# Layer A's third and fourth values unit as seven Strassen products, with sums made ahead

## The chip, the cores and the metric

One Trainium2 chip, one of its cores. The metric is the device time of one execution in microseconds; the median of three runs is given, and one further execution was taken with the hardware profiler. All matrix work runs on TensorE (PE), which keeps its order of instructions as the program wrote it; VectorE (DVE), ScalarE (ACT), GpSimd (POOL) and the queue of SyncE (SP) do the same with theirs.

## The reference

Two attention layers on 2048 rows of 1024 channels, 32 heads of 32, in float32; the outputs stand side by side.

```python
# layer A: a dilated window of 8 keys, step 2
qkv = (x @ wqkv).reshape(B, S, 3, H, Dh)
idx = pos[:, None] - off[None, :]            # off = 0, 2, ..., 14
logits = einsum("bhsd,bhswd->bhsw", q, kg) * Dh ** -0.5
o = einsum("bhsw,bhswd->bhsd", softmax(logits), vg)
a = o.reshape(B, S, D) @ wo
# layer B: causal, the last 256 keys
scores = einsum("bhqd,bhkd->bhqk", q, k) * Dh ** -0.5
b = einsum("bhqk,bhkd->bhqd", softmax(masked scores), v).reshape(B, S, D) @ wo
out = concatenate([a, b], -1)
```

## The kernel before

**Units.** The 2 x 2048 rows are cut into eight units of 512: units 0 to 3 are layer B (dense attention), units 4 to 7 layer A (windows). Each unit needs queries and keys (`qk_items`: eight slots s = 0..7 of four heads, two products each of 24 matmuls), values (`v_items`), attention (`attention`, `window`) and the output projection. Every float32 operand is split into a high and a low float32r part (`Stream.parts`: a cast on ACT or DVE, then one subtraction on DVE for each 512 columns), and a product is three matmuls: high x high, high x low, low x high.

**Who sets the order.** The Python code holds a planner: a clock with costs of its own (`Clock`), one list of matrix work `gemm` in the order of `plan`, and lists of attention work. Its loop takes from these whatever the clock says is ready first, and what it takes goes into the program in that order. Work for other engines is put into their queues when the clock passes a due time (`ck.defer`). Whatever a constant moves there, it moves the order of instructions of every engine after it. The chip doesn't know the clock: there each engine waits at the head of its queue.

**Weights and other operands.** `items` is the one sequence of 512 KB loads, issued on POOL's queue (L176) into three `raw` tiles; a tile is loaded again when its split is done. Some items have a gate: they are loaded only when the planner believes that their data stand in DRAM.

**Values before (L556 to 634).** Each unit makes its values as 512 x 1024 by 1024 x 1024, in three parts: part 0 (slots 0 to 3 of the attention) by 96 matmuls of 512 columns, parts 1 and 2 (slots 4, 5 and 6, 7) by 96 matmuls of 256 columns each; nine items of weights. A window unit has part 0 in slot 0, part 1 in slot 5 and part 2 in slot 7 (`V_SLOTS`). A finished bank is copied to `vbuf` by ACT or DVE (L621, L624).

**Strassen products before.** The output projection of layer A is made at the end, two units together, as seven products of half size in place of eight (`PRODUCTS`, `product`), 48 matmuls each: first units 4 and 5, then 6 and 7. Their sums of attention outputs (`sd`) and of weights (`td`) are made in the background: `background` (L845) reads two tiles of 512 KB on SP, runs four additions of 128 x 512 on DVE (L860), writes 2 x 512 KB back (L866). Two such tasks may run at once, in slots 4 to 7 of a pool of ten tiles `r`. The additions are put into DVE's queue 1.5 us (`BG_SLACK`) after the planner's landing time of the loads. Eight of these tasks concern outputs and four the weights `wo` (`weight_sums`).

**Windows.** For each slot of a layer A unit: scores (128 small matmul records into `s`), mask, maximum, exponent, sum and transpose (L946 to L976 on DVE), spreading on ACT (L985, L988), the product with the values into `o`, and a copy to `r` (L1047) that is written to DRAM as `od`. Queries and keys reach their seats `pbuf` by DMAs on SP's queue.

**Dense rows.** In units 0 to 3, `log_sum` (L1123) makes a small tile `hl` on DVE, and one matmul `s<-ident,hl` turns it.

Of the kernel before, what the change touches and what calls it, by code (L numbers as in the profile page):

```python
# [7 lines left out]
F32 = mybir.dt.float32  # L8
# [22 lines left out]
EXTRA, EACH = 246, 5.2  # L31
P_LATE = 1.5
VPARTS = ((0,4),(4,2),(6,2))
V_SLOTS = {0:0,5:1,7:2}
# [4 lines left out]
PRODUCTS = (("11", "11"), ("12", "21"), (0, 3), (2, 2), ("22", 1), (3, 0), (1, "22"))  # L39
PAIRS = (6,)  # L40
O_LATE = {4: {2: (0, 1), 3: (2, 3)}, 5: {2: (4, 5), 3: (6, 7)}}
O_AT = {}
BG_REST, BG_SLACK = 2.0, 1.5
C1, C3, CG, CV = 0.108, 0.2, 0.231, 0.242
# [192 lines left out]
def kernel(ctx, tc, xs, wqk, wv, wo, outs, units):  # L237
# [38 lines left out]
    for u in range(U):  # L276
        for s in range(NG):
            if 0 < u <= DU:
                plan += [("o", u - 1, n) for n in (O_SLOTS if u < DU else O_LATE[u]).get(s, ())]
            elif u in O_LATE:  # L280
                plan += [("o", DU - 1, n) for n in O_LATE[u].get(s, ())]
            if (u, s) in O_AT:
                plan.append(("p", DU, O_AT[u, s]))
            plan.append(("qk", u, s))
            vs = V_SLOTS if u else V0_SLOTS
            if s in vs:
                plan.append(("v", u, vs[s]))
        if u + 1 < U:
            plan.append(("x", u + 1))
# [3 lines left out]
    sd = {u: dram.tile([P, 4, 4, S], F32, name=f"sd{u}") for u in range(DU, U, 2)}  # L293
    td = dram.tile([P, 4, 4, S], F32, name="td")
    done = {}
    for k in ("stack", "v", "o", "ot", "out", "nat", "second", "clear", "scores", "s", "t"):
        done[k] = {}
# [5 lines left out]
    def product_items(u, i):  # L303
# [12 lines left out]
        for j in range(2):  # L316
            key = ("p", u, i, "t", j)
            if isinstance(b, str):
                n, c = 4 * (int(b[1]) - 1) + 2 * j, S * (int(b[0]) - 1)
                item(key, "w", wo[units[u][0], n:n + 2, :, c:c + S].rearrange("n p c -> p n c"))  # L320
            else:
                item(key, "w", td[:, b, 2 * j:2 * j + 2, :])
                gates[where[key]] = landed("t", 2 * j, 2 * j + 1)

# [13 lines left out]
    for p in plan:  # L338
# [3 lines left out]
        elif p[0] == "p":  # L342
            product_items(p[1], p[2])
        elif p[0] == "v":
            s0, n = VPARTS[p[2]]
# [23 lines left out]

    st.gates = gates  # L370
    where_o = {"ot": 0, "s": 0, "bg": 0}

# [105 lines left out]
    def qk_items(u, s):  # L478
# [100 lines left out]
        for t in range(2):  # L579
# [15 lines left out]
            def run(k, t=t, h=h):  # L595
# [6 lines left out]
                then = where["qk", u, s, t] + 1  # L602
                if k == ASK and then < len(st.items) and st.items[then][0] != "x":
                    st.split_to(then + 1)
                if k in (4, 6) and then < len(st.items) and st.items[then][0] in ("xw", "xt"):
                    st.split_to(then + k // 2)
# [100 lines left out]
    def o_items(u, n):  # L707
# [27 lines left out]
        def after(k):  # L735
            if k == NK - 1:
                done["out"][u, n] = True
                for f in list(stores.values()):
                    f()
                if u == DU - 1 and n == NG - 1:  # L740
                    ck.defer(ck.now + 3.0, weight_sums)
                o = stp.tile([P, S], F32, tag="ost", name="ost")
# [11 lines left out]

    held, totals = {}, {}

    def product(u, i):
# [38 lines left out]
        def after(n, k):  # L796
# [11 lines left out]
            def store(r, col, tile, e):  # L808
                def go():
                    nc.scalar.dma_start(outs[ORDER[u + r], 4 * col + n], tile)  # L810
                    ck.load("store", e)
                ck.defer(e, go)

            if i in (1, 4):
                where_o["ot"] += 1
                o = band[where_o["ot"] % 2][:, 1024:1536] if where_o["ot"] % 3 else stp.tile([P, S], F32, tag="ost", name="ost")
            if i == 0:
# [26 lines left out]

    bg = {"tasks": [], "idle": [0, 1]}  # L845

    def background():
# [28 lines left out]

        ck.defer(e + BG_SLACK, add)
        background()
# [4 lines left out]

    def weight_sums():
        w = wo[units[DU][0]]
        for n in range(4):
            task([(2 * i, w[n + 4 * i].rearrange("p (a b) -> p a b", a=2)) for i in range(2)],
                 ((0, 2, 0, ALU.subtract), (2, 3, 2, ALU.subtract), (3, 3, 0, ALU.subtract), (1, 1, 3, ALU.subtract)),
                 td[:, :, n, :], "t", n)

    def output_sums(u, k):
        task([(2 * r, od[u + r][:, k::4, :]) for r in range(2)],
             ((3, 2, 3, ALU.add), (2, 0, 2, ALU.subtract), (0, 3, 0, ALU.subtract), (1, 1, 0, ALU.subtract)),
             sd[u][:, :, k, :], "s", (u, k))
# [137 lines left out]
    def clear(buf):  # L1032
# [7 lines left out]
        done["clear"][buf] = ck.use("pool", 2.5, ck.now)  # L1040

    def finish(u, s, h):
        hg = u * NG + s
        done["o"][hg] = ck.now
        if u >= DU:
            o = slot(2 + hg % 2)[:, :S]
            nc.scalar.copy(o, h["o"])  # L1047
# [33 lines left out]
    def attention(u, s):  # L1081
# [43 lines left out]
        def log_sum():  # L1125
# [4 lines left out]
            def parts():  # L1130
# [135 lines left out]
    for p in plan:  # L1266
# [18 lines left out]
        elif p[0] == "p":  # L1285
            gemm += product(p[1], p[2])
    gemm = [Item(r, lambda run=run, after=after: (run(), after)[1], c) for r, run, c, after in gemm]

# [86 lines left out]
```

## Time and profile before

| | us |
|---|---|
| median of three runs (lowest, highest) | 1815.52 (1812.15, 1817.01) |
| the profiled execution, own time | 1813.28 |
| span of its trace | 1811.5 |
| PE busy | 1788.4 |
| DVE busy | 1265.9 |
| ACT busy | 918.4 |
| POOL busy | 410.0 |

The span runs from the first instruction to the last; 1.8 us of the execution's own time lie around it. PE's busy time counts pipelined matmuls from their start to a modelled end, so what one matmul costs in a stream is read from the distance of starts. By the copies L1047, which end each window, unit 4 runs from about 1033 us, unit 5 from 1175, unit 6 from 1353, unit 7 from 1513, and from 1671 only Strassen products are left.

### The profile page before, as it was taken

The numbers are of one execution on the slowest core, as the hardware profiler recorded it, in microseconds if no ns is written. First come the engines' busy times: TensorE is split into PE (matmuls) and PEld (weight loads), VectorE is DVE, ScalarE is ACT, GpSimd is POOL, SyncE is SP. The second block draws the span as 40 slices with busy tenths as digits, with TensorE's granted clock in tenths as the row PEclk, the third lists the DMA queues.
The fourth block names the chain that finished last, engine by engine and source line by source line (L and its number), as shares of the span: only waits on it lengthen the run. The fifth ranks groups of instructions, "written<-read, shape, count | busy, mean of one in ns | idle before, by whom it ended". The sixth has DMA issues, their size and how long they took to land. (4 is left out here: it accounts for less than half of the span.)

```text
span 1811.5 us, 38626 instructions
## 1 busy us (share of the span) xinstructions
PE 1788.4 (99%) x14730; PEld 1461.1 (81%) x14730; DVE 1265.9 (70%) x2794; ACT 918.4 (51%) x2297; POOL 410.0 (23%) x950
## 2 busy tenths in 40 slices
PE   8999999999999999999999999999999999999999
PEld 6787777888777888778887788888888878888887
DVE  6677876768867769767678566646765767558866
ACT  5556466555656565656655344423542534345342
POOL 2313423222242223332224300101010011002220
PEclk9999999999999999999999999999999999999999
DMA  8455664645646556554636353546753675448884
GB/s 244 114 146 134 184 167 137 168 137 138 184 140 175 148 138 172 139 157 138 152 111 172 99 153 107 174 131 215 238 181 110 196 248 161 129 148 300 304 271 145
DMA packets 129240, 303.60 MB, mean 168 GB/s; under 512 B 16160, under 2 KB 31520, under 8 KB 129056
## 3 DMA queue, kind: packets, MB, share of 16 engines
q0 software_dynamic: 45216, 164.65, 30.4%
q1 hardware_dynamic: 73472, 116.56, 22.9%
q10 hardware_dynamic: 10368, 19.93, 3.0%
q8 instruction: 117, 1.92, 0.5%
q14 instruction: 67, 0.55, 0.1%
HBM read 189.79 MB, written 44.04 MB: 129 GB/s over the span
## 5 line engine op out<-in xcount | busy, mean ns | idle before, releaser
L269 PE MATMUL g<-x,w 128*128 128x512 f32 x3744 | 927.1, 394 | 7.5 <-DVE w L227 4.6
L269 PEld LDWEIGHTS g<-x,w 128*128 128x128 f32 x3744 | 692.8, 189 | 145.6 <-issue 6.6
L269 PE MATMUL g<-w,x 128*128 128x256 f32 (+1 forms) x2304 | 391.4, 320 | 0.4 <-DVE w L227 0.2
L227 DVE TENSOR_TENSOR w<-raw,w 128x512 fp32r<-128x512 f32 x518 | 339.6, 697 | 34.3 <-ACT w L221 27.5
L269 PEld LDWEIGHTS g<-w,x 128*128 128x128 f32 x2304 | 332.3, 190 | 28.5 <-issue 1.7
L1114 ACT ACTIVATE s<-s,nm 128x384 f32<-128x384 f32 (+2 forms) x512 | 274.6, 537 | 101.5 <-DVE nm L1109 101.3
L1109 DVE CUSTOM_DVE_ANT_0 s<-s,mask_d 128x384 f32<-128x384 f32 (+2 forms) x512 | 261.8, 555 | 88.0 <-PE s L269 87.4
L1173 POOL TENSOR_SCALAR_AFFINE_SELECT pbuf<-pbuf 128x128 f32<-128x128 f32 (+1 forms) x606 | 220.2, 391 | 325.9 <-ACT pbuf L1194 324.5
L1194 ACT ACTIVATE pbuf<-s 128x384 f32<-128x384 f32 (+2 forms) x480 | 202.9, 505 | 72.2 <-PE s L269 70.7
L269 PE MATMUL g<-r,w 128*128 128x512 f32 x768 | 191.5, 394 | 1.5 <-ACT r L1069 0.7
L269 PEld LDWEIGHTS g<-r,w 128*128 128x128 f32 x768 | 141.8, 188 | 31.3 <-DVE r L1073 1.6
L176 POOL DMA_DIRECT2D raw<-wqk x126 | 68.2, 541 | 434.4 <-DVE w L227 316.0
L224 DVE CAST w<-raw 128x1024 fp32r<-128x1024 f32 x196 | 135.6, 692 | 32.7 <-PE g L269 29.5
L269 PEld LDWEIGHTS s<-qst,kst 128*128 128x128 f32 x704 | 113.1, 188 | 40.8 <-ACT s L1114 16.3
L269 PE MATMUL s<-kst,qst 96*128 96x384 f32 (+2 forms) x512 | 142.6, 342 | 1.0 <-ACT s L1114 0.6
L269 PE MATMUL s<-qst,kst 128*128 128x256 f32 (+2 forms) x704 | 136.5, 302 | 3.5 <-ACT s L1114 3.0
L946 DVE TENSOR_TENSOR band<-s,near 128x160 f32<-128x160 f32 x128 | 32.5, 317 | 119.4 <-PE s L269 119.4
L269 PEld LDWEIGHTS s<-kst,qst 96*128 96x128 f32 x512 | 93.4, 189 | 26.1 <-issue 4.4
L1114 ACT ACTIVATION_READ_ACCUMULATOR s<-s,nm 128x1 f32 x512 | 105.4, 206 | 0.0
L176 POOL DMA_DIRECT2D raw<-wv x72 | 45.9, 638 | 237.5 <-DVE w L227 155.8
L985 ACT COPY wide<-band 32x512 f32<-32x512 f32 x128 | 79.0, 617 | 40.1 <-DVE band L976 37.9
L269 PE MATMUL o<-pbuf,vbuf 128*32 128x384 f32 (+2 forms) x1408 | 92.2, 391 | 0.0
(79 smaller groups left out, 1258.6 us busy)
## 6 DMA issues: line engine op xcount, KB each, us to landing
raw<-wqk POOLq DMA_DIRECT2D x126, 512.0 KB, 4.4
raw<-wv POOLq DMA_DIRECT2D x72, 512.0 KB, 5.1
qst<-nat SPq DMA_DIRECT2D x96, 256.0 KB, 4.7
kst<-nat SPq DMA_DIRECT2D x96, 256.0 KB, 5.8
raw<-wo POOLq DMA_DIRECT2D x44, 512.0 KB, 4.5
raw<-xs POOLq DMA_DIRECT2D x28, 512.0 KB, 4.7
outs<-ost ACTq DMA_DIRECT2D x37, 256.0 KB, 2.7
kst<-halo SPq DMA_DIRECT2D x72, 128.0 KB, 4.5
```

What stands on the lines that cost most here:

```text
L176: (self.nc.scalar if early else self.nc.gpsimd).dma_start(raw if len(ap.shape) == 2 else raw.rearrange("p (a b) -> p a b", a=2), ap)
L224: nc.vector.tensor_copy(t[:, 0, :], raw)
L227: nc.vector.tensor_tensor(t[:, 1, c:c + 512], raw[:, c:c + 512], t[:, 0, c:c + 512].bitcast(F32), op=ALU.subtract)
L269: nc.tensor.matmul(out, left, right, **k)
L946: nc.vector.tensor_tensor(p64()[:, j, :, 24:], banks[j][0][:, :160].rearrange("p (b c) -> p b c", b=4), m, op=ALU.add)
L985: nc.scalar.copy(diag[r:r + 32, :, :, c:c + 32], turned[r:r + 32, :, :, 1, :])
L1109: nc.vector.tensor_tensor_reduce(ps[:, :n], ps[:, :n], mask[:, cut:full], scale=-1.0, scalar=BIG, op0=ALU.add, op1=ALU.min, accum_out=nm)
L1114: nc.scalar.activation(ps[:, :n], ps[:, :n], AF.Exp, bias=nm, scale=-1.0, accum_out=sm)
L1173: nc.gpsimd.affine_select(w, w, pattern=[[0, m], [step, n]], compare_op=ALU.is_ge, fill=0.0, base=base, channel_multiplier=chan)
L1194: nc.scalar.activation(w, ps[:, :pack * n].rearrange("p (j n) -> p j n", j=pack), AF.Exp)
```

## The change

The values of units 6 and 7 are made together as seven Strassen products in place of `v_items`: left operands are quarters of the two units' `x` or sums of them, right operands quarters of `wv` or sums of them. Products 0 and 1 stand in slot 0 of unit 6, product 2 in slot 1, 5 in slot 2, 6 in slot 3, 3 in slot 7, and 4 in slot 0 of unit 7 (`VP_AT`). Results gather in four `r` tiles and go by DVE additions into `vbuf`; the right half of unit 7 goes through DRAM (`vd`) and is read back by SP (`value_load`).

The sums for it, and the weight sums `td` that the background made, are made by a chain of 24 steps (`half_sums`) that starts with the end of the dense layer: four loads of 128 KB on SP into one tile, `VSLACK` = 5 us after their planned landing four additions of 128 x 256 on DVE, one store of 512 KB on SP, then the next step. Eight steps make `tv` (sums of `wv`), eight `sx` (sums of `x`), eight `td`.

Three further edits: `HL_LATE` puts the turning matmul of `hl` 0.8 us later in the planner's time; the output sums of units 4 and 5 begin only when product 3 of the values is through, with 8 us (`BG_EARLY`) in place of 1.5 between planned landing and additions; the copies of finished windows use one `r` tile in two halves in place of two tiles.

```diff
+HL_LATE = 0.8
+VPAIR = 6
+VP_AT = {(6, 0): (0, 1), (6, 1): (2,), (6, 2): (5,), (6, 3): (6,), (6, 7): (3,), (7, 0): (4,)}
+SUMS_FROM = 31
+VREST, VLAST, VNEED, VSLACK = 0.5, 2.0, 3.0, 5.0
...
-BG_REST, BG_SLACK = 2.0, 1.5
+BG_REST, BG_SLACK, BG_EARLY = 2.0, 1.5, 8.0
...
-            if s in vs:
+            if s in vs and u < VPAIR:
                 plan.append(("v", u, vs[s]))
+            plan += [("vp", u, i) for i in VP_AT.get((u, s), ())]
...
+                if kinds[:1] == ["xw"] and k in (0, 2, 4, 6):
+                    st.split_to(then + 1 + k // 2)
...
+    def value_product(i):
...
+        def run(n, k):
+            if k == 0:
+                h["ps"], h["b"] = rg.take()
+            x, w = left(k)[0], fetch("t", k // 2)[0]
...
+            for t, (y, z) in enumerate(TERMS):
+                mm(h["ps"], x[:, y, P * n:P * n + P], w[:, z, k % 2], start=(k == 0 and t == 0),
+                                 stop=(k == 3 and t == 2))
...
+        def after(n, k):
...
+            elif i == 3:
+                e = add(c, c)
...
+                    nc.scalar.dma_start(vd[:, n, :], c)
...
+                e = add(a, a)
+                if n == 3:
+                    bg["idle"] += [0, 1]
+                    ck.defer(ck.now + 3.0, background)
...
+    def half_sums(i=0):
...
+        t = slot(3).rearrange("p (a s) -> p a s", a=4)
+        for c in range(4):
+            nc.sync.dma_start(t[:, c, :], loads[c])
+            e = ck.copy("part", ck.now)
+
+        def add():
+            for to, x, y, op in ops:
+                nc.vector.tensor_tensor(*[t[:, c, :] for c in (to, x, y)], op=op)
+                e = ck.use("dve", 0.36, ck.now, port=True)
+            ck.defer(e, put)
+
+        def put():
+            nc.sync.dma_start(dst[:, :, k, 256 * z:256 * z + 256], t)
+            e = ck.copy("load", ck.now)
+
+            def end():
+                done[key][who] = ck.now
+                st.load_to(st.wanted)
+                half_sums(i + 1)
+
+            ck.defer(e + VREST, end)
+
+        ck.defer(e + VSLACK, add)
+
+    bg = {"tasks": [], "idle": []}
...
-        ck.defer(e + BG_SLACK, add)
+        ck.defer(e + (BG_EARLY if key == "s" and who[0] < PAIRS[0] else BG_SLACK), add)
...
-            o = slot(2 + hg % 2)[:, :S]
+            if "o" not in fin:
+                fin["o"] = slot(2)
+            o = fin["o"][:, S * (hg % 2):S * (hg % 2) + S]
...
-                aux.append(Item(lambda: latest(rs.when(BANK_LATE), e2), lambda: rows(hl), 0.08))
+                aux.append(Item(lambda: latest(rs.when(BANK_LATE), e2 + HL_LATE), lambda: rows(hl), 0.08))
```

What this does to the queues, at three places. The names: `g` is a bank of the projections' sums, `x` a unit's rows, `w` a split weight, `r` a tile of the pool of ten (a left operand that is a sum, in the change), `s` scores, `o` attention outputs, `band` a window's work tile.

First PE before, unit 6, about slots 4 to 6: queries and keys (`g<-x,w`), windows, and part 1 of the values.

```order
L269 MATMUL g<-x,w 128x512 x39
L269 MATMUL s<-pbuf 32x40 x64
L269 MATMUL o<-wide,vbuf_123 32x136 x12
L269 MATMUL o<-wide,vbuf_123 32x128 x4
L269 MATMUL g<-x,w 128x512 x9
L269 MATMUL g<-w,x 128x256 x96
L269 MATMUL g<-x,w 128x512 x6
```

PE of the change, unit 6, slots 1 and 2: the second half of slot 1's queries and keys, product 2 with its left operand from `r`, slot 2's queries and keys, product 5.

```order
L276 MATMUL g<-x,w 128x512 x33
L276 MATMUL g<-w,r 128x512 x48
L276 MATMUL s<-pbuf 32x40 x64
L276 MATMUL g<-x,w 128x512 x48
L276 MATMUL g<-w,r 128x512 x6
L276 MATMUL o<-wide,vbuf_126 32x136 x12
L276 MATMUL o<-wide,vbuf_126 32x128 x4
L276 MATMUL g<-w,r 128x512 x33
```

The blocks of 96 matmuls of 256 columns are gone from units 6 and 7; blocks of 48 of 512 columns stand between the queries and keys of slots 0 to 3.

Then DVE before, unit 6 about slots 5 and 6: the background's additions L860 stand between a window's maximum and its sum, with a weight's subtraction (L227) behind them.

```order
L946 TENSOR_TENSOR band<-s,near 128x4x40 x4
L956 TENSOR_REDUCE nm<-band 128x16
L958 TENSOR_TENSOR band<-band,nm 128x16x40
L860 TENSOR_TENSOR r<-r 128x512 x4
L970 TENSOR_REDUCE sm<-band 128x16
L972 RECIPROCAL sm<-sm 128x16
L974 TENSOR_TENSOR band<-band,sm 128x16x40
L976 STREAM_TRANSPOSE band<-band 128x1024
L227 TENSOR_TENSOR w<-raw,w 128x512 x2
```

DVE of the change, unit 6 at the end, through product 3: a step of `half_sums` (L1040) among the splits of the product's operands and of unit 7's rows, with two additions (L946) for each of the product's four banks.

```order
L234 TENSOR_TENSOR r<-raw,r 128x512 x2
L1040 TENSOR_TENSOR r<-r 128x256 x4
L231 CAST w<-raw 128x1024
L234 TENSOR_TENSOR w<-raw,w 128x512 x2
L234 TENSOR_TENSOR r<-raw,r 128x512 x2
L1151 TENSOR_TENSOR band<-s,near 128x4x40 x4
L234 TENSOR_TENSOR w<-raw,w 128x512 x2
L538 MEMSET nat 128x8
L1161 TENSOR_REDUCE nm<-band 128x16
L1163 TENSOR_TENSOR band<-band,nm 128x16x40
L234 TENSOR_TENSOR w<-raw,w 128x512 x2
L234 TENSOR_TENSOR x<-raw,x 128x512 x2
```

The output sums of units 4 and 5 (`r<-r 128x512`) are no longer in unit 6; they stand in unit 7, after this place.

Last SP of the change, in unit 4: the chain's loads and stores stand among the seats' loads (`pbuf<-nat`) and the stores of attention outputs (`od`).

```order
L1035 DMA r<-wv 128x256 x4
L551 DMA pbuf<-nat 32x512 x4
L551 DMA pbuf<-nat 32x520 x4
L1266 DMA od_99<-r 128x512
L1045 DMA tv<-r 512x1x256
L551 DMA pbuf<-nat 32x512 x4
L1035 DMA r<-wv 128x256 x4
L551 DMA pbuf<-nat 32x520 x4
```

Before, SP carried in this stretch only the seats' loads and the `od` stores.

More of the change, by code (lines that the diff above doesn't have):

```diff
@@ L294 @@
     td = dram.tile([P, 4, 4, S], F32, name="td")
+    tv = dram.tile([P, 4, 4, S], F32, name="tv")
+    sx = dram.tile([P, 4, 4, S], F32, name="sx")
+    vd = dram.tile([P, 4, S], F32, name="vd")
     done = {}
-    for k in ("stack", "v", "o", "ot", "out", "nat", "second", "clear", "scores", "s", "t"):
+    for k in ("stack", "v", "o", "ot", "out", "nat", "second", "clear", "scores", "s", "t", "vs", "vw", "vd"):
         done[k] = {}
@@ L322, in product_items, with value_items @@
                 item(key, "w", td[:, b, 2 * j:2 * j + 2, :])
[L323 removed]
+                gates[where[key]] = landed("t", *[(k, z) for k in (2 * j, 2 * j + 1) for z in range(2)])
+    def value_items(i):
+        a, b = PRODUCTS[i]
+        for j in range(2):
+            both = [(k, z) for k in (2 * j, 2 * j + 1) for z in range(2)]
+            if not isinstance(a, str):
+                key = ("vp", i, "s", j)
+                item(key, "xw", sx[:, a, 2 * j:2 * j + 2, :])
+                gates[where[key]] = landed("vs", *both)
+            key = ("vp", i, "t", j)
+            if isinstance(b, str):
+                n = 4 * (int(b[1]) - 1) + int(b[0]) - 1
+                item(key, "w", wv[units[VPAIR][0], n:n + 3:2, :, S * j:S * j + S].rearrange("t p c -> p t c"))
+            else:
+                item(key, "w", tv[:, b, 2 * j:2 * j + 2, :])
+                gates[where[key]] = landed("vw", *both)
     def item(key, kind, ap):
@@ L370 @@
     st.gates = gates
+    firsts = {where["vp", i, "t", 0] for v in VP_AT.values() for i in v}
     where_o = {"ot": 0, "s": 0, "bg": 0}
@@ new lines, in value_load @@
+    def value_load(part):
+        u = VPAIR + 1
+        s0, n = VPARTS[part]
+        if (u, part) in done["v"] or len(done["vd"]) < 4 or \
+                any((u - 1) * NG + s not in done["o"] for s in range(s0, s0 + n)):
+            return
+        b = 0
+        while b < 4:
+            c = (4 * u + b) % 6
+            m = min(4 - b, 6 - c)
+            nc.sync.dma_start(vbuf[part][:, c:c + m, :], vd[:, b:b + m, P * (s0 % 4):P * (s0 % 4 + n)])
+            e = ck.copy("load", ck.now)
+            b += m
+        done["v"][u, part] = e + VNEED
```

146 lines of the change are left out of this document (130 added, 16 removed).

## The prediction

> **What bounds the kernel now.** I read the engines' busy times by stage first (units 4, 5, 6, 7, then the Strassen tail), then PE's waits, then PE's order of time around the one long wait. The table by stage, with columns length, PE, PEld, DVE, ACT, POOL, granted clock, DMA share and GB/s:
>
> ```profile
> 0.00:1033.00 1033.00, 1020.24 (x6144) 821.77 (x6144) 763.00 (x1955) 597.36 (x1709) 318.80 (x788) 1.00 0.56 151
> 1033.00:1175.00 142.00, 141.42 (x1893) 118.02 (x1897) 91.10 (x159) 62.40 (x122) 15.26 (x27) 1.00 0.50 150
> 1175.00:1353.00 178.00, 177.47 (x2125) 147.78 (x2118) 110.89 (x184) 70.86 (x134) 18.46 (x33) 1.00 0.59 188
> 1353.00:1513.00 160.00, 156.01 (x1954) 129.83 (x1955) 104.77 (x179) 65.79 (x128) 16.32 (x29) 0.99 0.59 189
> 1513.00:1671.00 158.00, 156.79 (x2024) 131.11 (x2023) 98.14 (x164) 71.38 (x135) 17.77 (x32) 1.00 0.55 179
> 1671.00:1811.00 140.00, 136.44 (x602) 112.61 (x600) 98.04 (x158) 50.64 (x71) 23.37 (x41) 1.00 0.71 245
> ```
>
> PE is busy in all but 0.6, 0.5, 4.0 and 1.2 us of the four window stages, so matmuls taken out shorten the span unless a wait takes their place. DVE is the engine next to it, at 763/1033 = 74% in the dense half and (91.1 + 110.9 + 104.8 + 98.1)/638 = 63% in the windows. PE's waits over the whole span are few:
>
> ```profile
> PE g L269 <- DVE w L227: 4.8, 4, 3.9
> PE s L269 <- ACT s L1114: 3.6, 5, 1.1
> PE s L269 <- DVE hl L1135: 2.4, 4, 1.3
> PE g L269 <- ACT x L221: 2.3, 1, 2.3
> PE s L269 <- DVE qst L1292: 1.5, 1, 1.5
> ```
>
> **The change, 1: matmuls.** Busy times of pipelined matmuls overlap, so I take distances of starts. PE in unit 6, part 0 of the values, then part 1, each with the row behind it:
>
> ```profile
> 1360.51 12.53 PE L269 MATMUL g<-w,x 128*128 128x512 f32 x54
> 1372.88 1.52 PE L269 MATMUL g<-x,w 128*128 128x512 f32 x6
> ...
> 1438.47 11.68 PE L269 MATMUL g<-w,x 128*128 128x256 f32 x96
> 1449.98 1.55 PE L269 MATMUL g<-x,w 128*128 128x512 f32 x6
> ```
>
> 512 columns cost 12.37/54 = 0.229 us, 256 columns 11.51/96 = 0.120 us. A unit's values are 96 wide and 192 narrow matmuls: 22.0 + 23.0 = 45.0 us, two units 90.0. Seven products of 48 wide ones are 336 x 0.229 = 76.9 us. The tail of the chain of waits gives the price of exactly such products:
>
> ```profile
> 1670.50 136.96 PE g L269 x603
> ```
>
> At 136.96/603 = 0.227 us they cost 76.3. I take the middle of 13.1 and 13.7: **-13.4 us**. Nothing else on PE is added: the order of the change has 240 matmuls fewer, 576 less 336. A product whose left operand is a sum reads it from an `r` tile; the projections of units 0 to 3 already stream against such tiles, and I give them no other price.
>
> **2: the long wait of unit 6 goes.** DVE and PE before it, then the stage around it in pieces:
>
> ```profile
> 1455.72 0.83 DVE L958 TENSOR_TENSOR band<-band,nm 128x640 f32<-128x640 f32 x1
> 1461.29 2.87 DVE L860 TENSOR_TENSOR r<-r 128x512 f32<-128x512 f32 x4 [4.74 <-DMA r<-od]
> ...
> 1467.24 1.25 DVE L227 TENSOR_TENSOR w<-raw,w 128x512 fp32r<-128x512 f32 x2
> ```
>
> ```profile
> 1453.76 10.27 PE L269 MATMUL g<-x,w 128*128 128x512 f32 x44
> 1467.94 6.24 PE L269 MATMUL g<-x,w 128*128 128x512 f32 x19 [3.91 <-DVE w L227]
> 1474.12 1.12 PE L269 MATMUL o<-wide,vbuf 128*32 128x136 f32 x32
> ```
>
> ```profile
> 1464.00:1468.00 4.00, 0.09 (x2) 0.06 (x1) 3.90 (x7) 0.87 (x3) 0.00 (x0) 1.00 0.96 320
> 1468.00:1472.00 4.00, 4.00 (x12) 3.18 (x13) 3.90 (x8) 3.06 (x8) 1.06 (x2) 0.66 0.75 220
> ```
>
> DVE stood 4.74 us at the head of its queue for a background load (`r<-od`); behind it lay the four additions (2.87), the rest of a window, and at last the subtraction of the weight that PE needed. PE waited 3.91 us, and then the granted clock was 0.66: 19 matmuls took 1474.12 - 1467.94 = 6.18 us for 19 x 0.227 = 4.31, so another 1.9 us. The change moves these tasks out of unit 6 and gives them 8 us instead of 1.5: **-5.8 us**. How late such loads can be, the issues and the waits show (KB each, median us to landing; then DVE's waits for them, us and times):
>
> ```profile
> r<-od SPq DMA_DIRECT2D x16, 512.0 KB, 7.3
> r<-wo SPq DMA_DIRECT2D x8, 512.0 KB, 4.9
> td<-r SPq DMA_DIRECT2D x8, 512.0 KB, 6.4
> kst<-halo SPq DMA_DIRECT2D x72, 128.0 KB, 4.5
> ...
> DMA r<-od: 19.9, 4
> ```
>
> All four waits of DVE fell on `r<-od`, none on `r<-wo`, and one of the four stopped PE for long. The page on "TensorE: Matmul & The Clock Gate", section "What's actually happening", in the Trainium skill says that an idle window of about 3.4 us halves PE's clock until it has been busy as long; by it alone an estimate of the surcharge is 1.7 us in place of 1.9, and the trace agrees.
>
> **3: the turning matmul.** PE waited 2.4 us in four places for `hl`; 0.8 us later in the planner's time covers the three short ones and most of the long one. The dense half is set in another order by it, which can cost as much elsewhere. Bounds -2.4 and +2.4; I take half, **-1.2 us**.
>
> **4: what DVE and SP get.** The rows of DVE operations:
>
> ```profile
> L860 DVE TENSOR_TENSOR r<-r 128x512 f32<-128x512 f32 x48 | 33.2, 691 | 21.1 <-DMA r<-od 19.9
> L805 DVE TENSOR_TENSOR r<-g,r 128x512 f32<-128x512 f32 x40 | 26.9, 689 | 23.5 <-PE g L269 23.5
> L1176 DVE TENSOR_TENSOR pbuf<-pbuf,keep_d 128x256 f32<-128x256 f32 x33 | 13.9, 445 | 31.6 <-ACT pbuf L1194 31.4
> L224 DVE CAST w<-raw 128x1024 fp32r<-128x1024 f32 x196 | 135.6, 692 | 32.7 <-PE g L269 29.5
> L227 DVE TENSOR_TENSOR w<-raw,w 128x512 fp32r<-128x512 f32 x518 | 339.6, 697 | 34.3 <-ACT w L221 27.5
> ```
>
> The chain adds 24 x 4 additions of 256 columns, 96 x 0.445 = 42.7 us, and takes away the four weight tasks, 16 x 0.691 = 11.1. The products' results cost, per bank of four, additions in products 1, 2, 4 and 5, two in 3, and two halves in 6: 24 x 0.689 + 8 x 0.445 = 20.1 us, in place of copies that mostly were ACT's. Operands are 22 items in place of 18; four more splits cost up to 4 x (0.692 + 2 x 0.697) = 8.3. Together DVE gets about +60 us in units 4 to 7: (405 + 60)/(638 - 18) = 75%. That is what it carries in the dense half, where PE still lost only 1033 - 1020.24 = 12.8 us, of which 2.3 + 1.5 were the very start (the waits for the first `x` and `qst`). On the average, then, DVE hides it behind PE's matmuls. What counts is where it comes in lumps. In each of slots 1, 2 and 3 of unit 6, and in slot 7, within about 48 matmuls (11 us) DVE must make two left sums' halves and two weights (8 subtractions, 5.6 us, and casts that ACT may share), 4 to 8 additions of results (2.8 to 5.5 us) and a window's mask to transpose (about 6 us); the two last weights are split only from the sixth of the eight steps before the product. In slot 7 unit 7's rows come on top. If the cover is gone there, the first matmul of a product waits, with everything behind it on PE.
>
> No row shows this. From below it is 0: of the tail's 603 matmuls, with the same splits and additions but few windows, none waits visibly. From above, each of the seven products could pay what the worst place paid, 3.9 + 1.9: 40.6 us. The nearest row is the dense half with the same DVE load: 12.8 us less 3.8 for the start in 1033, so 0.9 per 100 us; over 620 us 5.4, where the windows lost 638 - 631.7 = 6.3 with the long wait and 2.4 without. That is +3. SP's queue gets 108 issues more (120 of the chain and 4 for `vd`, 16 fewer for the weight tasks), and a store of the chain (`td<-r` landed in 6.4) is waited for at the head of the queue by the next loads; the seats' loads (`pbuf<-nat`) and `od` stores lie behind it, for whom scores and the last products wait. The median `r<-wo` of 4.9 us leaves the chain's additions well inside the 5 us of slack that they get beyond the planned landing. The chain moves 24 MB where the weight tasks moved 8: 16 MB over 620 us are 26 GB/s on top of the 150 to 189 of the window stages, where 320 were reached for a moment. I add 1: **+4 us**, between 0 and 40.6.
>
> **The sum.** -13.4 - 5.8 - 1.2 + 4 = -16.4. Against the profiled execution's own 1813.28 this is 1796.9. The median of the runs shown, 1815.52, lies 2.2 above that execution; I put the forecast where the median would be: **1799**.
>
> The last products keep their start. When the last additions of the background ran, the line's own view tells:
>
> ```profile
> L860 DVE TENSOR_TENSOR r<-r x48: 683/691/695, 1251.9 to 1707.2; 128x512 f32<-128x512 f32 x48
> ```
>
> That is 36 us after the last window (1671), with a store of about 6 behind. The five products that need these sums are the last 240 matmuls. Before, 603 - 240 = 363 matmuls (82 us) lay between the last window and them; by the order of the change 549 stand behind the last window, so 309 (70 us).
>
> **Rivals.**
> A. Nothing new waits and both old waits go whole: -13.4 - 5.8 - 2.4 = -21.6, so 1794. For it: DVE at 75% in the dense half. Against: the lumps above.
> B. The starts of products wait, each 1 to 2.5 us: +7 to +17 in place of +4, so 1802 to 1812. For it: PE's only long wait before was for just such a split.
> C. Slower: DVE's queue is the bound in unit 6. A wait for a DMA or a window stands ahead of the splits at every product, PE stops for 3.9 us and pays 1.9 more in clock; seven of these are 40.6, less 20.4: +20, so 1835. It decides from 20.4/7 = 2.9 us per product. The row for it is DVE's 4.74 us wait, which became 3.91 of PE's; against it, three of DVE's four such waits cost PE next to nothing.
> D. The change doesn't shorten PE: excluded for the count, but the time can come back if the attention of unit 7, with fewer matmuls to hide behind, ends later against the tail. 70 us of cover against some 42 needed speak against it; it would end near 1815.
>
> The clock gate of the page named above, as a mechanism here: waits over 3.4 us are charged again, which is C's price; many short ones (B) are not.
>
> **How the numbers follow.** Forecast (1796 to 1804) 0.45, A 0.15, B 0.17, D 0.05, C 0.18. A difference of 0.3% (5.4 us) is about what a measurement of this kernel can tell from no change: faster means under 1810.1, slower over 1821. Faster: forecast, A and most of B, 0.74. Same: the rest of B, D and the mildest of C, 0.10. Slower: 0.16. The range from 1792 to 1818 leaves out part of A below and C above.
>
> **What would show it.** Right: PE with 240 instructions fewer; no wait of PE near 4 us in unit 6 and no granted clock under 0.9 there; DVE near 75% in the window stages; PE's idle time in units 4 to 7 near 6 us; the waits for `hl` under 1 us. Wrong: waits of PE for DVE's `w` or `r` at the first matmuls of products 2, 5, 6 and 3; DVE waiting for `r<-wv`, `r<-xs` or `r<-wo`; PE waiting for `pbuf<-nat`, which would be SP's queue. What would make the forecast wrong most of all is a planner whose DVE costs are below the traced ones (0.61 us in its code for an operation of 0.69), since then lumps that it takes for covered are not.

## The result, and the profile after

The change runs at **1810.65 us** (median of 20 runs, 1808.46 to 1815.28) against 1815.32 (20 runs, 1807.30 to 1820.62) for the kernel before on the same chip: ratio 0.998, 95% interval 0.9971 to 0.999. It is faster, by 4.7 us where 16.4 were forecast: the interval leaves out 1, though 1810.65 is above the 1810.1 under which the prediction would have called it faster. The profiled execution of the change took 1810.36 us, with a span of 1808.5.

The page of the change: PE's busy time, then what was moved.

```profile
PE 1779.4 (98%) x14490; PEld 1439.0 (80%) x14490; DVE 1294.4 (72%) x2879; ACT 935.2 (52%) x2319; POOL 417.7 (23%) x967
...
DMA packets 154649, 324.57 MB, mean 179 GB/s; under 512 B 18016, under 2 KB 58976, under 8 KB 154464
```

PE's busy time fell by 9.0 us, from 1788.4, and its idle time (span less busy) rose by 6.0, from 23.1 to 29.1. The stages of the change, with the same columns as in the prediction: the dense half, units 4, 5, 6, 7, and the Strassen products at the end.

```profile
0.00:1038.00 1038.00, 1021.53 (x6143) 821.54 (x6143) 756.75 (x1939) 596.12 (x1710) 325.02 (x801) 1.00 0.55 151
1038.00:1183.00 145.00, 142.99 (x1903) 118.68 (x1900) 100.53 (x185) 65.30 (x126) 14.72 (x26) 1.00 0.66 198
1183.00:1363.00 180.00, 178.95 (x2116) 147.30 (x2116) 112.91 (x201) 75.16 (x140) 18.43 (x34) 1.00 0.63 193
1363.00:1543.00 180.00, 175.66 (x1950) 140.37 (x1950) 130.62 (x238) 80.56 (x146) 21.51 (x40) 1.00 0.68 213
1543.00:1680.00 137.00, 135.41 (x1840) 108.14 (x1836) 103.59 (x173) 70.48 (x132) 16.22 (x29) 1.00 0.75 246
1680.00:1808.00 128.00, 124.85 (x557) 102.94 (x549) 90.01 (x145) 47.53 (x67) 21.83 (x38) 1.00 0.74 255
```

Read the first row first. The 6144th matmul of PE's order started at 1032.5 us and starts at 1038.8 now: the dense half, which the products do not touch, has lost 6.3 us. In the four window stages PE is idle 2.0, 1.1, 4.3 and 1.6 us where it was 0.6, 0.5, 4.0 and 1.2. Unit 6 lost its long wait and is idle as long as before. PE's waits of the change, first over the whole span, then in unit 6 alone (us, times, longest):

```profile
PE s L276 <- ACT s L1328: 4.6, 7, 1.1
PE s L276 <- DVE hl L1349: 3.7, 3, 1.5
PE g L276 <- ACT w L228: 2.2, 3, 1.1
...
PE s L276 <- DVE qst L1363: 1.3, 3, 0.5
```

```profile
PE g L276 <- ACT w L228: 1.6, 2, 1.1
PE o L276 <- ACT wide L1193: 1.0, 1, 1.0
PE g L276 <- DVE nat L538: 0.8, 1, 0.8
PE g L276 <- DVE x L234: 0.6, 1, 0.6
PE g L276 <- DVE w L234: 0.3, 1, 0.3
```

One wait of 3.9 us has become six of 0.3 to 1.1, at other operands.

For a sum by stage, count matmuls in PE's order. The first 6144 are the dense half, the first 10162 are that and units 4 and 5; up to there both kernels run the same matmuls, in another order.

| us | before | change | difference |
|---|---|---|---|
| to the start of the 6145th (dense half) | 1033.2 | 1039.5 | +6.3 |
| from there to the start of the 10163rd (units 4 and 5) | 321.9 | 324.9 | +3.0 |
| from there to the end (units 6 and 7, last products) | 456.4 | 444.2 | -12.2 |

The change has 144 matmuls of 512 columns more and 384 of 256 fewer. At the forecast's 0.227 us and 0.120 us that is the -13.4 of the forecast, and the median distances of starts are 0.227 to 0.228 and 0.120 us in the change too. With the long wait of unit 6 and the slow clock behind it, forecast at -5.8, the last row should be -19.2. It is -12.2, so 7.0 us came back there, and another 9.3 were lost ahead of the first product.

### The profile page after: what moved, and what is told of

The parts are those of the page before. It is cut to its first block, busy times and chain, and to the rows that moved or that the text cites. A ratio compares the mean times of both kernels' runs of the same rounds, so it can differ in the third digit from the quotient of the medians.

```text
span 1808.5 us, 38436 instructions
## 1 busy us (share of the span) xinstructions
PE 1779.4 (98%) x14490; PEld 1439.0 (80%) x14490; DVE 1294.4 (72%) x2879; ACT 935.2 (52%) x2319; POOL 417.7 (23%) x967
## 5 line engine op out<-in xcount | busy, mean ns | idle before, releaser
L234 DVE TENSOR_TENSOR w<-raw,w 128x512 fp32r<-128x512 f32 x510 | 334.6, 697 | 51.7 <-ACT w L228 45.6
L276 PE MATMUL g<-w,x 128*128 128x256 f32 (+1 forms) x1872 | 332.8, 327 | 0.9 <-DVE w L234 0.7
L276 PEld LDWEIGHTS g<-w,x 128*128 128x128 f32 x1872 | 276.7, 190 | 28.1 <-DVE w L234 2.2
L1387 POOL TENSOR_SCALAR_AFFINE_SELECT pbuf<-pbuf 128x128 f32<-128x128 f32 (+1 forms) x619 | 226.0, 393 | 300.9 <-ACT pbuf L1408 299.5
L231 DVE CAST w<-raw 128x1024 fp32r<-128x1024 f32 x176 | 122.1, 694 | 27.2 <-PE g L276 26.8
L228 ACT CAST w<-raw 128x1024 fp32r<-128x1024 f32 (+1 forms) x80 | 82.7, 1038 | 75.8 <-PE g L276 29.0
L1363 DVE TENSOR_TENSOR qst<-s,pick 32x512 fp32r<-32x512 f32 x128 | 79.3, 676 | 12.8 <-PE s L276 12.0
```

The lines of the kernel that those rows point to most:

```text
L228: nc.scalar.copy(t[:, 0, :], raw)
L231: nc.vector.tensor_copy(t[:, 0, :], raw)
L234: nc.vector.tensor_tensor(t[:, 1, c:c + 512], raw[:, c:c + 512], t[:, 0, c:c + 512].bitcast(F32), op=ALU.subtract)
L276: nc.tensor.matmul(out, left, right, **k)
L1363: nc.vector.tensor_tensor(q[96:P, j, :].rearrange("p (b s) -> p b s", s=P), ps[0:32, None, 0:P].to_broadcast([32, 4, P]), cst["pick"][0:32 ...
L1387: nc.gpsimd.affine_select(w, w, pattern=[[0, m], [step, n]], compare_op=ALU.is_ge, fill=0.0, base=base, channel_multiplier=chan)
```

## The experiments

Each was run beside the kernel before (medians of 1813.3 to 1815.1 us in the four groups), so that ratios are compared. My theory from this profile: the delayed turning matmul costs, and the rest is given back by the chain's DVE additions in lumps. The rival: the re-set order of all the queues costs, whatever work is in them.

**The edits apart.** e1 is the change with `HL_LATE` at zero, e2 the kernel before with it, e3 the kernel before with the longer slack alone, e4 the chain without the products. e4 has `HL_LATE` at zero too; its output sums of units 4 and 5 begin in unit 6 again, as before, and the change's other edits stay.

```diff
-HL_LATE = 0.8
+HL_LATE = 0.0
```

> The change with HL_LATE = 0: up to the end of the dense half every engine's order is that of the kernel before. Theory 1 (the later turning matmul re-sets the dense half and costs some 6 us there; the windows and values cost some 10 more than without waits): about 9 us faster than before, ratio about 0.995, end of the dense half near 1032 us as before, not 1038. Theory 2 (the 6 us of the dense half are chance of one execution, and the whole loss is DVE's load in the windows): the time of the change itself, about 4.7 us under before, ratio 0.997 to 0.998, and an end of the dense half that differs by under 2 us from the change's.

e1: 1805.32 us, ratio 0.9959 (0.9944 to 0.9974). It beats the change and the kernel before.

```diff
+HL_LATE = 0.8
...
-                aux.append(Item(lambda: latest(rs.when(BANK_LATE), e2), lambda: rows(hl), 0.08))
+                aux.append(Item(lambda: latest(rs.when(BANK_LATE), e2 + HL_LATE), lambda: rows(hl), 0.08))
```

> The kernel before with nothing but HL_LATE = 0.8: its dense half has the order of the change's. Theory 1: about 6 us slower than before, ratio 1.003, end of the dense half near 1038 us, and waits of PE for hl that are not shorter than before (3.7 us in three places as in the change). Theory 2: within 2 us of before; my prediction had 1.2 us faster.

e2: 1817.71, ratio 1.0024 (1.0013 to 1.0035). The delay is a loss of 4.4 us alone, and of 3.8 in the change (0.998 against 0.9959).

```diff
-        ck.defer(e + BG_SLACK, add)
+        ck.defer(e + (BG_EARLY if key == "s" and who[0] < PAIRS[0] else BG_SLACK), add)
```

> The kernel before with only the 8 us between landing and additions for the output sums of units 4 and 5. Theory 1: the 3.9 us wait in unit 6 and its slow clock go, 4 to 6 us faster than before, ratio about 0.997, DVE's waits for r<-od in unit 6 under 1 us. Rival: the wait is not there in every execution of the kernel before (its runs spread over 13 us), so on the median less is won, 0 to 3 us.

e3: 1810.62, ratio 0.9987 (0.9976 to 0.9998). The slack is worth 2.4 us (0.4 to 4.4 by the interval), not 5.8. In its trace the wait of 3.9 us is gone, and a new one of 1.6 us for ACT's cast of a weight stands a slot later:

```profile
PE g L269 <- ACT w L221: 1.6, 1, 1.6
```

```diff
-VP_AT = {(6, 0): (0, 1), (6, 1): (2,), (6, 2): (5,), (6, 3): (6,), (6, 7): (3,), (7, 0): (4,)}
+VP_AT = {}
...
-            if s in vs and u < VPAIR:
+            if s in vs:
```

> The change with HL_LATE = 0 and with the values of units 6 and 7 as before (nine items of weights, 576 matmuls); the chain of 24 steps runs in full, the sums tv and sx are made and not used, td is used. It prices the chain and the 8 us slack alone. Theory 1: the chain costs PE some 3 us in units 4 and 5, and the wait in unit 6 goes (-5.8): 0 to 3 us faster than before. Rival (the chain costs nothing, the loss of units 6 and 7 lies in the products): 5 to 6 us faster than before. A third (the chain with its queue on SP and DVE is the main loss): 3 us slower or more.

e4 (against e1): 1815.01, ratio 1.0005 (0.9995 to 1.0015). Against e3, which has the same slack, the chain costs (1.0005 - 0.9987) x 1814 = 3.3 us. Against e4, the products of e1, with the output sums' move to unit 7, gain (1.0005 - 0.9959) x 1814 = 8.3, where their matmuls save 13.4.

**What of the chain costs.** e5 is e1, and e6 is e4, without the 96 additions of the chain, the order unchanged. e7 holds the chain's `td` steps back until product 6 is through.

```diff
-                nc.vector.tensor_tensor(*[t[:, c, :] for c in (to, x, y)], op=op)
```

> e1_hl0 with the 96 additions of the chain left out on DVE (tv, sx and td hold unsummed quarters); the planner's clock is charged as if they were there, so every other instruction stands in the same order. e1_hl0 was 0.9959 of before. If DVE's 40 us of additions are what delays the splits (theory 1): PE's waits at products 2, 5 and 6 shrink from 7.7 us of excess to under 4, and the whole is 4 to 6 us faster than e1_hl0, ratio about 0.993. Rival (late raw loads and the casts behind them delay the splits, the additions only stand in between): within 1.5 us of e1_hl0.

> e4_chain_only with the chain's 96 additions left out in the same way: the chain's loads and stores alone. e4_chain_only was 1.0005, the slack alone (e3_slack8) 0.9987, so the chain costs about 3.3 us. If the additions are its price: ratio 0.9987, as e3_slack8. If the DMAs and SP's queue are: 1.0005, as e4_chain_only.

> e1_hl0 with the chain's remaining td steps held back from the end of unit 5 until product 6 of the values is through. Theory 1 (additions in unit 6 stand in front of the splits): 2 to 4 us faster than e1_hl0, ratio about 0.994. Rival (raw loads are late whether or not the chain runs): within 1.5 us of e1_hl0, or slower, since the steps then meet the output sums of units 4 and 5 in unit 7.

e5: 1807.19, ratio 0.9957 (0.9941 to 0.9974), as e1. e6: 1819.35, ratio 1.0024 (1.001 to 1.0038), not below e4. So the additions, 40.5 us of DVE in the change's profile where 42.7 were forecast, cost nothing that the runs can tell, and my reason for the lumps fell. e7: 1810.34, ratio 0.9974 (0.9965 to 0.9984), if anything slower than e1.

e9 leaves out the loads, additions and stores of the chain's sixteen steps for `tv` and `sx` too, but charges them to the planner.

```diff
-            nc.sync.dma_start(t[:, c, :], loads[c])
+            if i >= 16:
+                nc.sync.dma_start(t[:, c, :], loads[c])
```

> This is e4 (the chain, values by plain matmuls, turning matmul undelayed) with the loads, additions and stores of the chain's sixteen steps for tv and sx left out, but charged in the planner's time, so that everything else stands in the same order; nothing in e4 or here uses those sums. Theory, the chain costs what its transfers do on SP's queue and in DRAM: the price of 3.3 us disappears and the ratio is near e3's 0.9987. Rival, the chain costs what the re-set order of units 4 to 7 does: the ratio stays at 1.0005 to 1.0024, where e4 and e6 were.

e9: 1815.34, ratio 1.0006 (0.9997 to 1.0016), the same as e4. The chain's work in those steps costs nothing that the runs can tell; **that the planner knows of it** does. In the profiles, the stretch from the 6145th matmul to the 10163rd takes 320.3 to 322.0 us in the five kernels without the chain (before, e2, e3, e10, e16) and 324.0 to 328.0 in the thirteen with it; in e9, which issues the chain's first real load only at 1324.8, it takes 324.7. The edit to the copies of finished windows is in all thirteen too, but in e9 no such copy waits for a transfer there. The place can be seen. PE at the end of unit 4 in e3, in the order of before:

```profile
1163.34 5.73 PE L269 MATMUL g<-x,w 128*128 128x512 f32 x24
1168.91 3.56 PE L269 MATMUL g<-w,x 128*128 128x512 f32 x15
...
1173.46 6.41 PE L269 MATMUL g<-w,x 128*128 128x512 f32 x27
```

The same place in e9, whose chain moves no data there, and in e4, whose chain does:

```profile
1163.38 6.03 PE L276 MATMUL g<-x,w 128*128 128x512 f32 x24 [0.70 <-ACT w L228]
1169.25 3.56 PE L276 MATMUL g<-w,x 128*128 128x512 f32 x15
...
1173.79 2.56 PE L276 MATMUL g<-w,x 128*128 128x512 f32 x10
1176.84 3.51 PE L276 MATMUL g<-w,x 128*128 128x512 f32 x14 [0.49 <-DVE w L234]
```

```profile
1164.65 6.03 PE L276 MATMUL g<-x,w 128*128 128x512 f32 x24 [0.70 <-ACT w L228]
...
1178.11 3.49 PE L276 MATMUL g<-w,x 128*128 128x512 f32 x14 [0.49 <-DVE w L234]
```

The waits of 0.70 and 0.49 us stand at the same instructions with and without the transfers, and not in the other order. What differs is the engine that casts the weight (`Stream.parts` gives the cast to the engine that would end it first by the planner's clock, with a bias). The weight of the first wait in e3, then in e9:

```profile
1162.05 0.69 DVE L224 CAST w<-raw 128x1024 fp32r<-128x1024 f32 x1
1162.77 1.29 DVE L227 TENSOR_TENSOR w<-raw,w 128x512 fp32r<-128x512 f32 x2
```

```profile
1161.66 0.60 ACT L527 ACTIVATE nat<-g 128x512 f32<-128x512 f32 x1 [0.54 <-PE g L276]
1162.29 1.05 ACT L228 CAST w<-raw 128x1024 fp32r<-128x1024 f32 x1
```

On ACT the cast stands behind a copy that waited for PE, and it takes longer: it ends at 1163.34 in place of 1162.74, and PE starts at 1163.38. The weight of the second wait is cast on DVE in e3 too (1173.14) and on ACT in e9 (1174.41). The two waits are 1.2 of the chain's 3.3 us. From 1033 to 1353 us ACT casts 18 of 52 weights in e3, and 23 of 51 in e4 and e9. The change has both waits:

```profile
1172.33 6.01 PE L276 MATMUL g<-x,w 128*128 128x512 f32 x24 [0.57 <-ACT w L228]
...
1185.77 3.51 PE L276 MATMUL g<-w,x 128*128 128x512 f32 x14 [0.49 <-DVE w L234]
```

**What of the products costs.** e8 gives products 2, 5 and 6 a quarter of `x` that is there already in place of a sum as left operand.

```diff
+VPRODUCTS = tuple(("11" if i in (2, 5, 6) else a, b) for i, (a, b) in enumerate(PRODUCTS))
...
-        a, b = PRODUCTS[i]
+        a, b = VPRODUCTS[i]
```

> e1_hl0 with a quarter of unit 6's own rows as left operand of value products 2, 5 and 6 in place of a sum (part of the values is then not the reference's): six items of 512 KB with their splits fewer, matmuls the same, sx still made. Theory 1 and its rival both allow that the supply of split operands is the bound at these products: excess there falls from 7.7 us in three slots to about 3, and the kernel is 4 to 5 us faster than e1_hl0, ratio about 0.9935. If PE waits there for something else (windows, result additions): within 1.5 us of e1_hl0.

e8: 1800.28, ratio 0.9923 (0.9908 to 0.9938), 5.0 us below e1 by the medians and 6.5 by the ratios. But it also has another order, and takes away loads, casts and subtractions together. e13 to e15 take these away in the order of e1, in all four products that have a sum on the left (2, 3, 5 and 6); e11 splits earlier.

```diff
-                if kinds[:1] == ["xw"] and k in (0, 2, 4, 6):
-                    st.split_to(then + 1 + k // 2)
+                if kinds[:1] == ["xw"] and k in (0, 2, 4):
+                    st.split_to(then + 2 + k // 2)
...
-                if kinds == ["w", "xw"] and k == 6:
+                if kinds == ["w", "xw"] and k == 4:
```

> This is e1 with the operands of the value products split a step or two earlier in the product ahead. Theory, the products of unit 6 wait because the three raw tiles come free too late, held by splits that stand behind a window's work on DVE: the waits at the products' starts get shorter and the time falls by 2 to 4 us from e1, a ratio near 0.994. Rival, the splits are late since the loads are, or DVE's queue is full anyway: no change from e1 (0.996), or slower, since earlier splits push the windows back.

```diff
+            if self.items[self.loaded][0] == "xw" and self.loaded < self.wide:
+                self.nc.gpsimd.dma_start(raw.rearrange("p (a b) -> p a b", a=2)[:, :, :128], ap[:, :, :128])
```

> This is e1 with the loads of the sums that are left operands of the value products cut from 512 KB to 128 KB (the casts and subtractions read the loaded quarter repeatedly, so left operands are wrong copies of it); the order of every engine is that of e1. Theory 1, the products wait because these loads come late or take bandwidth from others: most of the 5 us that e8 gained come back, a ratio near 0.993. Theory 2, DVE's subtractions, or theory 3, the order itself: no change from e1, 0.996.

```diff
+            if not (self.items[self.split][0] == "xw" and self.split < self.wide):
                 nc.vector.tensor_tensor(t[:, 1, c:c + 512], raw[:, c:c + 512], t[:, 0, c:c + 512].bitcast(F32), op=ALU.subtract)
```

> This is e1 without the subtractions on DVE that split those sums (24 of 128 x 512 at about 0.69 us, charged in the planner's time as before; the products read the high half three times). Theory 1, loads: no change from e1, 0.996. Theory 2, DVE's queue behind these subtractions is what PE waits for: most of the 5 us come back, near 0.993. Theory 3, order: no change.

(The change's trace shows 16 such subtractions, not the 24 that I wrote.) e15 leaves out the load and the casts as well, under the same condition.

> This is e1 without loads, casts and subtractions of those sums, all charged in the planner's time, so that the order stays that of e1 (the products read their split weights as left operands as well). Theories 1 and 2: the whole gain of e8 comes back, a ratio near 0.992. Theory 3, what e8 gained was another order and not the work that it left out: no change from e1, 0.996.

| | us | ratio (95% interval) |
|---|---|---|
| e11 | 1806.31 | 0.9955 (0.9941 to 0.9969) |
| e13 | 1806.03 | 0.9957 (0.9945 to 0.9969) |
| e14 | 1803.84 | 0.9948 (0.9935 to 0.9961) |
| e15 | 1803.31 | 0.9947 (0.9932 to 0.9961) |

Earlier splits and shorter loads change nothing. Without the subtractions, or without all of that work, e1 gains 2.0 and 2.2 us by the ratios, inside the intervals; the other 4.3 of e8's 6.5 appear only when the planner re-sets the order. So the larger part seems to be order again, the smaller perhaps the work on the sums; but the intervals of e8 and e15 touch, and how the price of the products divides between the two stays open.

Where that price falls is open too. From the 10163rd matmul to the end, the profiles of e1, e5 and e13 (products, one order up to there) take 445.0 to 445.7 us and those of e4, e6 and e9 (none) 455.9 to 458.7, so 10.2 to 13.7 of the 13.4 us are gained there. The dense half, written in the order of before in all of them, took 1028.7 to 1033.2 us in the five such profiles without products and 1031.9 to 1036.4 in the nine with. That is one execution of each, and nothing here shows why.

One product of the change lost 2.2 us in three waits (0.30 + 1.08 + 0.83). PE at product 6, and DVE ahead of it:

```profile
1442.94 1.43 PE L276 MATMUL g<-w,r 128*128 128x512 f32 x5 [0.30 <-DVE w L234]
1444.30 1.12 PE L276 MATMUL o<-wide,vbuf 128*32 128x136 f32 x32
1446.49 0.50 PE L276 MATMUL g<-w,r 128*128 128x512 f32 x1 [1.08 <-ACT w L228]
1447.82 7.53 PE L276 MATMUL g<-w,r 128*128 128x512 f32 x32 [0.83 <-DVE nat L538]
```

```profile
1438.53 1.25 DVE L1181 STREAM_TRANSPOSE band<-band 128x1024 f32<-128x1024 f32 x1
1439.70 1.25 DVE L234 TENSOR_TENSOR r<-raw,r 128x512 fp32r<-128x512 f32 x2
...
1442.80 1.80 DVE L1040 TENSOR_TENSOR r<-r 128x256 f32<-128x256 f32 x4
...
1446.47 1.29 DVE L234 TENSOR_TENSOR w<-raw,w 128x512 fp32r<-128x512 f32 x2 [0.67 <-ACT w L228]
```

POOL's queue issues the load of the weight, and ACT casts it:

```profile
1441.24 0.72 POOL L183 DMA_DIRECT2D raw<-wv  x1 [7.55 <-DVE r L234]
```

```profile
1443.59 1.14 ACT L228 CAST r<-raw 128x512 fp32r<-128x512 f32 x2
1445.40 1.04 ACT L228 CAST w<-raw 128x1024 fp32r<-128x1024 f32 x1 [0.67 <-DMA raw<-wv]
```

The sum's subtraction stood behind a window on DVE until 1439.70; the raw tile came free after it, so the weight's load began at 1441.24, its cast at 1445.40, its subtraction at 1446.47. PE waited for both (the wait named `nat` ends with this subtraction; L538 is the 0.07 us behind it on DVE). The four additions of a chain step at 1442.80 delayed nothing here: DVE stood idle for 0.67 us before the subtraction, until ACT's cast was there.

But the late load is the smaller part. In e14, without the sum's subtraction, the load begins at 1432.94, and PE still waits 0.89 and 0.83 us at this place. ACT in e14:

```profile
1438.37 0.29 ACT L1195 COPY wide<-band 32x128 f32<-32x128 f32 x1
1438.69 1.14 ACT L228 CAST r<-raw 128x512 fp32r<-128x512 f32 x2
1439.73 1.04 ACT L228 CAST w<-raw 128x1024 fp32r<-128x1024 f32 x1
```

The weight's cast stands behind the eight copies of a window and the two casts of the next sum. In e15, without those casts as well, 0.75 us of waiting is left.

**The old slack in the change.** e12 is e1 with the 1.5 us of before.

```diff
-BG_REST, BG_SLACK, BG_EARLY = 2.0, 1.5, 8.0
+BG_REST, BG_SLACK, BG_EARLY = 2.0, 1.5, 1.5
```

> This is e1 with the 1.5 us of before in place of 8 between the planned landing and the additions of the output sums of units 4 and 5; the order is that of e1 up to unit 7 and differs only there. Theory, the slack is worth its 2.4 us (e3) here too: a ratio near 0.998, with DVE waits for od in unit 7. Rival, in the change these sums stand in unit 7, where PE has nothing waiting behind them: no change from e1, 0.996.

e12: 1807.70, ratio 0.9965 (0.9952 to 0.9978): not told apart from e1. DVE's wait for these loads over the whole span, in the change and in e12, against 19.9 us before:

```profile
DVE r L1072 <- DMA r<-od: 2.4, 1, 2.4
```

```profile
DVE r L1072 <- DMA r<-od: 0.5, 1, 0.5
```

In the change the move to unit 7 removes the wait; the slack adds nothing.

**The delay's size.** e10 and e16 are e2 with 0.4 and 1.2 us.

```diff
-HL_LATE = 0.8
+HL_LATE = 0.4
```

> The kernel before with the turning matmul 0.4 us later in place of 0.8 (e2). Theory, the delay itself is what costs, through PE's order in the dense slots: about half of e2's price, a ratio near 1.001. Rival, any value sets the dense half in another order and its price is that order's accident: the ratio may lie anywhere from 0.998 to 1.004, without relation to the size of the delay.

> The kernel before with the turning matmul 1.2 us later (0.4 cost 0.5%, 0.8 cost 0.2%). Theory, each value re-sets the dense half and its price is that order's own: the ratio lies between 0.998 and 1.006 with no trend over 0.4, 0.8, 1.2. Rival, from some size on the delay covers the wait for hl and gains: under 0.998; or the delay costs by its size: over 1.006.

e10: 1823.93, ratio 1.0054 (1.004 to 1.0069). e16: 1821.96, ratio 1.0048 (1.0035 to 1.0062). So 0.4, 0.8 and 1.2 us cost 0.54%, 0.24% and 0.48%: no trend, and half the delay costs twice as much. The dense half of e10, and of e12, which has no delay:

```profile
0.00:1041.00 1041.00, 1022.18 (x6143) 822.02 (x6143) 767.58 (x1983) 597.76 (x1707) 311.88 (x761) 1.00 0.54 150
```

```profile
0.00:1033.00 1033.00, 1019.75 (x6144) 821.80 (x6144) 762.88 (x1956) 597.31 (x1709) 319.30 (x788) 1.00 0.55 151
```

The same matmuls end 8 us later. PE's waits between 30 and 1030 us, before and in e10:

```profile
PE s L269 <- ACT s L1114: 3.6, 5, 1.1
PE s L269 <- DVE hl L1135: 2.4, 4, 1.3
PE g L269 <- DVE r L1073: 0.4, 2, 0.2
...
```

```profile
PE s L270 <- ACT s L1115: 5.0, 8, 1.2
PE s L270 <- DVE hl L1136: 3.3, 2, 2.1
PE s L270 <- DMA kst<-nat: 1.9, 1, 1.9
PE g L270 <- DVE w L228: 1.5, 3, 0.7
PE s L270 <- ACT pbuf L1195: 1.1, 2, 0.7
PE s L270 <- DVE qst L1150: 0.8, 2, 0.6
...
```

With the smaller ones they sum to 7.1 us before and 13.8 in e10: 6.7 of the 8 us. The other profiles agree: 6.5 and 8.3 us in e1 and e12, whose dense half has the order of before, and 11.6, 11.9 and 12.6 in e2, the change and e16. The waits for `hl` themselves did not shrink with the delay: 1.9 to 3.6 us in the three without it, 1.8 to 3.7 in the four with it. What the delayed orders add are longer waits for ACT's `s` (4.6 to 5.5 us where 3.6 and 3.7 were) and waits that the others do not have, for `qst` (0.8 to 2.4) and for transfers into `kst` and `halo` (0.8 to 1.9).

## Why the prediction was wrong

**Step 1, matmuls, -13.4: right.** The count is as forecast, and the 192 matmuls that read `r` start 0.227 us apart by the median, the ordinary price. That alone says nothing of the products' net worth, which is 8.3.

**Step 2, the long wait, -5.8: the mechanism right, the size wrong.** No wait near 4 us is left in unit 6, and the granted clock there is 1.00; the longest wait is 1.1 us. (The page "TensorE: Matmul & The Clock Gate", section "What's actually happening", of the Trainium skill has PE's clock halved after an idle window of about 3.4 us; waits of up to 1.1 us with the clock at 1.00 agree.) But taking the wait away alone (e3) is worth 2.4. I priced one place as if nothing else became late a slot further on; e3's profile shows 1.6 us there, and the 4.2 that this leaves of 5.8 lie inside e3's interval. Whether every execution of the kernel before has the long wait, which I had named as a rival for e3, was not tested. That the profiled execution of before, with the whole wait in it, was 2.2 below its median should have warned me that the wait is no clean term.

**Step 3, the turning matmul, -1.2 between -2.4 and +2.4: wrong in sign and outside its bounds.** It costs 3.8 to 4.4. This is the largest single miss, 5.0 of the 12.8 us between -16.4 and the -3.6 below. I bounded the cost of another order by the waits that the edit aimed at, for which there was no reason: the order of the whole dense half was open, and e10 lost 0.54% by it. I had written "can cost as much elsewhere"; elsewhere is not bounded by here.

**Step 4, new waits, +4: measured 8.4**, 3.3 for the chain and 13.4 - 8.3 = 5.1 that came with the products, inside its wide bounds. The reason that I gave, lumps on DVE, does not hold for the chain's additions (e5, e6), nor do SP's queue and the 16 MB of `tv` and `sx` (e9). One sign that I had named for a wrong forecast came, DVE waiting for the chain's loads (`r<-xs`, 7.0 us in two places), but kernels without these additions (e5, e6) or without these loads (e9) are no faster. DVE in the window stages is busy (100.5 + 112.9 + 130.6 + 103.6)/642 = 70%, against a forecast of 75%. What costs in the chain is that the queues of units 4 and 5 are written in another order, with more of the weights cast on ACT. At the products the work on the sums as left operands is worth some 2 us, not told apart from nothing; the rest of their price stays open.

**Sum:** -13.4 - 2.4 + 3.8 + 8.4 = -3.6, a ratio of 0.998, which is the change's. It must come out so, since each term begins at the ratio where the one before it ends (1, e3, e4, e1, the change); it divides the miss and does not test the division.

**Rivals.** B, short waits at the starts of products, came nearest (1802 to 1812); a part of its time fell in the dense half, though, for which it had no place. A had nothing new wait and both old waits go whole; the one of unit 6 went, that for `hl` did not, and new ones came. C's price per product, over 2.9 us, was reached nowhere in the change's profile; the most that one lost is the 2.2 of product 6. D did not happen: behind the last window PE is idle for 3.2 us, where it was 3.6.

Of the signs that I named, PE's 240 instructions fewer, the missing long wait and the clock came; the waits for `hl` (3.7, not under 1) and the idle time in units 4 to 7 (9.0, not 6) spoke against the forecast.

## What to carry to other kernels

Where a planner writes the order, a constant that shifts one small instruction re-sets everything behind it. Price such an edit by how much of the program it re-orders, not by the wait it is meant for, and try it alone. And count a removed wait at what is late next: here the saved time of matmuls came out as counted, and what rested on a single wait did not.

## What the runs showed that I had not expected

Half a delay cost more than the whole (0.54% at 0.4 us, 0.24% at 0.8, 0.48% at 1.2). Another 0.18%, between e3 and e4, stayed when most of the chain's transfers existed only in the planner's time (e9 and e4, 1.0006 and 1.0005). Which of the moved instructions starts the short waits in the dense half was not settled: the traces show where PE waits, and the runs only that the order decides it.
